# Five rearrangements at the edges of a kernel bound by TensorE: decayed attention, then a low-rank mixer and two large products

## The chip, the cores and the metric

The kernel runs on one core of a Trainium2 chip. The metric is the device time of one execution in microseconds; every time below is the median of several executions, with the range or a 95% interval where it matters. The first eight experiments ran on one chip, the last four on another, the kernel before each time in the same rounds; runs of different rounds are compared by their ratios to it, or in their traces. A profile is the record of one execution, and its span (from the first to the last instruction) is some 1.8 us shorter than the time of the same execution.

## The reference

```python
# q, k, v: (4, 8, 768, 64); lam: 8 numbers near 0.98; blocks of 64 positions
for b in range(nb):
    intra = einsum(qb, kb) * Dmask                 # lam**(i-j) for i >= j, else 0
    intra = einsum(intra, vb)
    inter = einsum(qb * lam**(pos + 1), kv_state)
    out[block] = intra + inter
    kv_state = lam**block * kv_state + einsum(kb * lam**(block-1-pos), vb)
x = out as (4, 768, 512)
u = x + V.T @ (U.T @ x)        # per batch, over the 768 positions; rank 32
result = u + relu(u @ w_ch1) @ w_ch2               # 512 -> 2048 -> 512
```

The large weights arrive as 64-bit floats, as pairs of 32-bit words, and VectorE and ScalarE turn them into 32-bit floats and then into high, low and difference parts. U and V come the same way.

## The kernel before

Attention runs in 24 steps of 128 positions (4 batches by 6, counted 0 to 23). In each step TensorE turns q and k (pq, pk), multiplies the masked scores by v (intra, into px), adds to the state (pkv), makes the scores of the next step (pss) and starts px of the next step from the state (inter). VectorE masks the scores and adds up the state kv, GpSimd scales q and k by powers of lam (qs, ks), and ScalarE copies the results of turning and of px out of PSUM. Pieces of work with the weights are dealt out to the steps as asides. The two large products, from about 163 us on, take four fifths of the time.

```python
pieces = [("prep", 0), ("scale", 0), ("scores", 0), ("inter", 0), ("masked", 0)]
for s in range(NS):
    ...
    step += [("intra", s), ("late", s), ("state", s)]
    step += [("turned", done - 1)] * (done > 0)
    step += [("scores", s + 1)] * more
    step += [("aside", s)] * (done >= 0)
    step += [("inter", s + 1), ("masked", s + 1), ("fade", s + 1)] * more
    step += [("aside", s)] * (done < 0)
...
def powers():                       # run before step 0
    ...
    for a in range(HP):
        nc.vector.tensor_tensor_scan(powq[:, a, :], lamh[:, a : a + 1].broadcast_to([P, P]),
            zeros.broadcast_to([P, P]), 1.0, ALU.mult, ALU.add)
...
def scores(s):
    for a in range(HP):             # 4 x 2 products of 64 x 128 weights
        for x in range(2):
            nc.tensor.matmul(out=pss[:, x, a, :], lhsT=kt[half[x], a, :],
                rhs=qt[half[x], a, :], start=True, stop=True)
...
for steps, at in (                  # which part of which weight in which step
    (u_side, (0, 2, 2, 3, 3)),
    (v_steps(), (1, 1, 3, 3, 4, 4, 4, 5, 5, 5)),
    (w1_steps(0, True), (3, 4, 5, 6, 7, 8, 9, 10, 12, 13, 14)),
    (w1_steps(1, True), (8, 9, 10, 11, 15, 16, 17, 18, 19, 20, 21)),
):
```

The first four entries of `w1_steps(0, True)` are four loads of one block of w_ch1; the fifth entry, step 7, begins to convert it.

## Time and profile before

| | value |
|---|---|
| time | 686.68 us, median of 3 (686.65 to 686.88) |
| span of the profiled run | 684.9 us, granted clock 0.995 |
| instructions | 12572, of which 4812 matmuls |
| attention | until about 132 us |
| largest wait of TensorE in it | 2.10 us at 33.7 us, for the state kv |
| load rate of the DMA engines, 0 to 50 us | 195 GB/s, 9.75 MB |

The prediction shows the lines that it rests on. Two readings became important only later. The first is a line from the page's table of DMA queues (queue and kind: packets, MB, share of the 16 engines' time). It counts the packets that fetch instructions:

```profile
q8 instruction: 38, 0.62, 0.4%
```

Each packet brings 16 KB of instructions; 19 of the 38 come in the first 130 us.

The second is the order of events of the kernel before (start, length, engine and line, what it does, how often; in brackets what the engine waited for):

```profile
8.03 2.22 POOL L371 TENSOR_TENSOR ks<-kraw,small 128x512 f32<-128x512 f32 x2 [6.72 <-DVE small L305]
...
14.26 2.08 PE L398 MATMUL pss<-qt,kt 64*128 64x128 f32 x16
...
16.27 0.85 PE L439 MATMUL px<-kv,qs 64*64 64x64 f32 x32
...
50.66 0.43 DVE L424 TENSOR_TENSOR kv<-pkv,faded 128x256 f32<-128x256 f32 x1 [0.94 <-PE pkv L416]
51.00 0.97 DVE L153 TENSOR_SCALAR sc<-words 128x512 uint32<-128x512 uint32 x1
```

The scans of lam's powers, 8.23 to 11.16 in the prediction's lines, stand almost wholly beside this GpSimd work. In front of inter(1) the second pss takes 2.08 instead of 1.16 us, in the half clock from 13.25 to 16.66. And at step 7, at 51.00, VectorE takes up the words of w_ch1 right behind the state: they had landed, but only at 50.77 by the trace, 0.2 us before they were wanted.

### The profile page before, as it was taken

The numbers are of one execution on the slowest core, as the hardware profiler recorded it, in microseconds if no ns is written. First come the engines' busy times: TensorE is split into PE (matmuls) and PEld (weight loads), VectorE is DVE, ScalarE is ACT, GpSimd is POOL, SyncE is SP. The second block draws the span as 40 slices with busy tenths as digits, with TensorE's granted clock in tenths as the row PEclk, the third lists the DMA queues.
The fourth block names the chain that finished last, engine by engine and source line by source line (L and its number), as shares of the span: only waits on it lengthen the run. The fifth ranks groups of instructions, "written<-read, shape, count | busy, mean of one in ns | idle before, by whom it ended". The sixth has DMA issues, their size and how long they took to land.

```text
span 684.9 us, 12572 instructions
## 1 busy us (share of the span) xinstructions
PE 675.0 (99%) x4812; PEld 547.1 (80%) x4812; DVE 499.4 (73%) x856; ACT 291.5 (43%) x543; POOL 114.1 (17%) x92
## 2 busy tenths in 40 slices
PE   8999999999999999999999999999999999999997
PEld 6878888887888888888888888888888888888885
DVE  5568898876999877777799255787586676775854
ACT  3657777644666544444456231232232322322320
POOL 3546566532000000000000000030030110300300
PEclk9999999999999999999999999999999999999999
DMA  9978886244577855655566989956353363453431
GB/s 206 208 171 218 217 214 157 78 169 169 186 256 248 266 201 206 206 203 207 194 239 236 329 301 372 331 159 193 94 193 114 105 201 95 147 166 101 156 92 62
DMA packets 131629, 131.24 MB, mean 192 GB/s; under 512 B 81330, under 2 KB 89522, under 8 KB 131570
## 3 DMA queue, kind: packets, MB, share of 16 engines
q1 hardware_dynamic: 130514, 130.18, 60.5%
q8 instruction: 38, 0.62, 0.4%
q10 hardware_dynamic: 1056, 0.26, 0.2%
q14 instruction: 21, 0.17, 0.1%
HBM read 80.09 MB, written 50.33 MB: 190 GB/s over the span
## 4 chain that ended last, share of the span: by engine, by line
PE 96%; DVE 2%; ACT 1%; issue 1%; DVEq 0%
PE pz L704 26%; PE pz L837 13%; PE pz L835 13%; PE pd L714 13%; PE pd L839 13%; PE px L451 3%; PE pss L398 3%; PE put L514 2%; PE px L439 2%; PE pq L353 1%; PE pkv L416 1%; PE pk L353 1%; PE pu L497 1%; PE pp L465 1%; PE pr L483 1%
## 5 line engine op out<-in xcount | busy, mean ns | idle before, releaser
L704 PE MATMUL pz<-u_hl,w 128*128 128x512 f32 x768 | 191.2, 398 | 0.2 <-ACT r L710 0.2
L704 PEld LDWEIGHTS pz<-u_hl,w 128*128 128x128 f32 x768 | 143.9, 188 | 36.4 <-issue 1.1
L835 PE MATMUL pz<-w_hl,m 128*128 128x512 f32 x384 | 151.6, 396 | 0.0
L837 PE MATMUL pz<-w_hl,m 128*128 128x512 f32 x384 | 151.6, 396 | 0.0
L839 PE MATMUL pd<-w_d,m 128*128 128x512 f32 x384 | 150.0, 396 | 0.0
L818 ACT ACTIVATE m<-mt 128x512 fp32r<-128x512 f32 x96 | 60.6, 632 | 196.3 <-PE pd L839 139.0
L819 DVE SCALAR_TENSOR_TENSOR m<-rm,m 128x512 fp32r<-128x512 f32 x96 | 71.4, 745 | 52.9 <-ACT m L818 52.7
L859 POOL TENSOR_TENSOR o<-o,u 128x512 f32<-128x512 f32 x20 | 29.8, 1525 | 447.5 <-DVE o L857 447.5
L719 DVE SCALAR_TENSOR_TENSOR r<-pd,r 128x512 f32<-128x512 f32 x96 | 61.8, 685 | 55.1 <-ACT r L710 45.5
L714 PE MATMUL pd<-u_d,w 128*128 128x512 f32 x384 | 98.2, 397 | 0.0
L837 PEld LDWEIGHTS pz<-w_hl,m 128*128 128x128 f32 x384 | 72.3, 188 | 17.7
L839 PEld LDWEIGHTS pd<-w_d,m 128*128 128x128 f32 x384 | 72.3, 188 | 17.7
L835 PEld LDWEIGHTS pz<-w_hl,m 128*128 128x128 f32 x384 | 72.3, 188 | 17.6
L714 PEld LDWEIGHTS pd<-u_d,w 128*128 128x128 f32 x384 | 72.2, 188 | 17.4
L710 ACT ACTIVATE r<-pz 128x512 f32<-128x512 f32 x96 | 51.9, 593 | 58.3 <-PE pz L704 58.2
L820 DVE SCALAR_TENSOR_TENSOR m<-m 128x512 fp32r<-128x512 f32 x96 | 69.1, 720 | 0.9
L817 DVE TENSOR_SCALAR mt<-rm 128x512 uint32<-128x512 uint32 x96 | 46.2, 481 | 27.2 <-DMA rm<-r_d 26.3
L204 ACT CAST w<-wt 128x512 fp32r<-128x512 f32 x32 | 19.9, 622 | 41.3 <-DVE wt L201 34.0
L407 DVE TENSOR_TENSOR sm<-pss,mask 128x512 f32<-128x512 f32 x48 | 30.7, 680 | 8.9 <-PE pss L398 8.9
L451 PEld LDWEIGHTS px<-vraw,sm 128*64 128x64 f32 x768 | 25.2, 141 | 9.1 <-issue 3.2
L382 POOL TENSOR_TENSOR qs<-qt,powq 128x512 f32<-128x512 f32 x20 | 25.5, 1277 | 33.4 <-ACT qt L356 24.9
L451 PE MATMUL px<-vraw,sm 128*64 128x64 f32 x768 | 28.7, 229 | 1.9 <-DVE sm L407 1.9
(88 smaller groups left out, 711.9 us busy)
## 6 DMA issues: line engine op xcount, KB each, us to landing
r_d<-r SPq DMA_DIRECT2D x96, 256.0 KB, 2.6
rm<-r_d SPq DMA_DIRECT2D x96, 256.0 KB, 2.7
words<-in_moe_w_ch_dram SPq DMA_DIRECT2D x30, 512.0 KB, 4.1
w_d<-w SPq DMA_DIRECT2D x16, 768.0 KB, 3.3
w_hl<-w_d SPq DMA_DIRECT2D x16, 512.0 KB, 6.2
vraw<-in_v_dram SPq DMA_DIRECT2D x24, 256.0 KB, 4.1
u_d<-x_nat SPq DMA_DIRECT2D x24, 256.0 KB, 3.4
u<-u_d SPq DMA_DIRECT2D x24, 256.0 KB, 4.1
```

The lines of the kernel that those rows point to most:

```text
L451: nc.tensor.matmul(out=px[half[t], x, a, :], lhsT=sm[:, x, a, half[t]], rhs=vr[:, 2 * a + x, :], start=(first and a == 0), stop=(a == HP - 1),
L704: nc.tensor.matmul(out=acc[g][0], lhsT=w[:, n, ct, :], rhs=uhl[g][:, n, ct, :], start=(ct == 0 and n == 0), stop=(ct == CT - 1 and n == 1),)
L710: nc.scalar.mul(rs[g], acc[g][0], 1.0 + E)
L714: nc.tensor.matmul(out=acc[g][1], lhsT=w[:, 2, ct, :], rhs=ud[g][:, ct, :], start=(ct == 0), stop=(ct == CT - 1),)
L719: nc.vector.scalar_tensor_tensor(rs[g], acc[g][1], 4096.0, rs[g], ALU.mult, ALU.add)
L817: nc.vector.tensor_scalar(t.bitcast(U32), r.bitcast(U32), HI, None, ALU.bitwise_and)
L818: nc.scalar.activation(out=m[:, 0], in_=t, func=AF.Relu)
L819: nc.vector.scalar_tensor_tensor(m[:, 1], r, 0.0, hi, ALU.max, ALU.subtract)
L820: nc.vector.scalar_tensor_tensor(m[:, 2], hi, E, low, ALU.mult, ALU.subtract)
L835: nc.tensor.matmul(out=pz, lhsT=m[:, 0, cols], rhs=hl[:, 0], start=first, stop=False)
L837: nc.tensor.matmul(out=pz, lhsT=m[:, 1, cols], rhs=hl[:, 1], start=False, stop=end)
L839: nc.tensor.matmul(out=pd, lhsT=m[:, 2, cols], rhs=dd, start=first, stop=end)
```

## The change

The intent is to take TensorE's waits and overhead out of the attention part, in five places. (1) lam is loaded first, and its powers, which only step 1 needs, are computed behind the mask of step 0. (2) U moves one or two steps forward, so that its conversions no longer stand in front of V's. (3) ScalarE's conversions of weights stand a step later everywhere, behind the copies that TensorE waits for. (4) Scores are made on 64x64 instead of 64x128 tiles, so that they and inter, which follows them, are in the same tiling mode. (5) The last sum and its store are done in two halves.

```diff
-                nc.tensor.matmul(
-                    out=pss[:, x, a, :], lhsT=kt[half[x], a, :], rhs=qt[half[x], a, :],
-                    start=True, stop=True,
-                )
+                for t in range(2):
+                    nc.tensor.matmul(
+                        out=pss[half[t], x, a, :], lhsT=kt[half[x], a, half[t]],
+                        rhs=qt[half[x], a, :], start=True, stop=True,
+                    )
     pieces = [("prep", 0), ("scale", 0), ("scores", 0), ("inter", 0), ("masked", 0)]
+    pieces += [("powers", 0)]
-        step += [("intra", s), ("late", s), ("state", s)]
-        step += [("turned", done - 1)] * (done > 0)
+        step += [("intra", s)] + [("late", s)] * (done < 0) + [("state", s)]
+        step += [("turned", done - 1)] * (done > 0) + [("late", s)] * (done >= 0)
-        (u_side, (0, 2, 2, 3, 3)),
-        (v_steps(), (1, 1, 3, 3, 4, 4, 4, 5, 5, 5)),
+        (u_side, (-1, 1, 1, 2, 2)),
+        (v_steps(), (0, 0, 3, 3, 4, 4, 5, 5, 5, 5)),
-        late[:] = [None] * (s < NT)
+        late[:] = [None]
+    nc.scalar.dma_start(out=lam_row[:, 0:H], in_=lam.unsqueeze(0))
     load_next("q", nc.sync)
     load_next("k", nc.scalar)
-    for name in "qkvkvqkv":
+    for name in "qkvkv":
+        load_next(name)
+    aside(-1)
+    for name in "qkv":
         load_next(name)
...  (two conversions of w_ch1 put into the late list; blank matmuls before and behind lam's product)
-        finish(NG - 1, n)
+        finish(NG - 1, n, [slice(0, C // 2), slice(C // 2, C)] if n == TG - 1 else [slice(0, C)])
```

More of the change, by code (lines that the diff above doesn't have):

```diff
@@ L203, in five @@
             )
-            nc.scalar.copy(o[:, 0, :], t)
+            on_scalar(lambda: nc.scalar.copy(o[:, 0, :], t))
         def six():
@@ L208, in six @@
             nc.vector.tensor_tensor(out=w, in0=w, in1=st["t"], op=ALU.subtract)
-            nc.scalar.mul(st["o"][:, 1, :], w, 4096.0)
+            on_scalar(lambda: nc.scalar.mul(st["o"][:, 1, :], w, 4096.0))
         def seven():
@@ L270, in load @@
             )
-            if name == "q" and s == 0 and h == 0:
-                engine.dma_start(out=lam_row[:, 0:H], in_=lam.unsqueeze(0))
         raw[s, name] = t
@@ L335, with keep_busy @@
     half = [slice(0, D), slice(D, P)]
-    def keep_busy():
+    def keep_busy(n, cols=P):
         out = one_bank([P, C], "idle", "pq")
-        for i in range(5):
-            nc.tensor.matmul(out=out[:, 0:P], lhsT=blank, rhs=blank, start=True, stop=True)
+        for i in range(n):
+            nc.tensor.matmul(
+                out=out[:, 0:cols], lhsT=blank, rhs=blank[:, 0:cols], start=True, stop=True
+            )
     qts, kts = {}, {}
@@ L360, in prep @@
             for name in "qk":
-                if (s, a0, name) != (0, 0, "q"):
-                    turn_half(s, a0, name)
+                turn_half(s, a0, name)
         st[s].update(qt=qts.pop(s), kt=kts.pop(s))
@@ L397, in scores @@
             for x in range(2):
-                nc.tensor.matmul(
-                    out=pss[:, x, a, :], lhsT=kt[half[x], a, :], rhs=qt[half[x], a, :],
-                    start=True, stop=True,
-                )
+                for t in range(2):
+                    nc.tensor.matmul(
+                        out=pss[half[t], x, a, :], lhsT=kt[half[x], a, half[t]],
+                        rhs=qt[half[x], a, :], start=True, stop=True,
+                    )
     def masked(s):
@@ L650 @@
     make_gather()
-    keep_busy()
-    turn_half(0, 0, "q")
+    keep_busy(2)
     pl = one_bank([P, H], "pl", "pt")
     nc.tensor.matmul(out=pl, lhsT=lam_row[:, H:], rhs=lam_row[:, 0:H], start=True, stop=True)
+    keep_busy(3)
     nc.vector.tensor_copy(out=lamb, in_=pl)
@@ L657 @@
     scale_k(0)
-    powers()
-    run.update(aside=aside, late=on_scalar_late)
+    run.update(aside=aside, late=on_scalar_late, powers=lambda s: powers())
     for what, s in pieces:
@@ L847, in residual, with finish @@
             nc.sync.dma_start(out=us[n], in_=u_d[g * TG + n])
-    def finish(g, n):
+    def finish(g, n, parts=[slice(0, C)]):
         pz, pd = acc.pop(n)
@@ L856, in finish @@
             nc.scalar.mul(o, pz, 1.0 + E)
-        nc.vector.scalar_tensor_tensor(o, pd, 4096.0, o, ALU.mult, ALU.add)
-        if g < NG - 1:
-            nc.gpsimd.tensor_tensor(out=o, in0=o, in1=u, op=ALU.add)
         s = g * TG + n
         b, c = divmod(s, NT)
-        nc.sync.dma_start(out=out[b, c * P : (c + 1) * P, :], in_=o)
+        for part in parts:
+            nc.vector.scalar_tensor_tensor(
+                o[:, part], pd[:, part], 4096.0, o[:, part], ALU.mult, ALU.add
+            )
+            if g < NG - 1:
+                nc.gpsimd.tensor_tensor(out=o, in0=o, in1=u, op=ALU.add)
+            nc.sync.dma_start(out=out[b, c * P : (c + 1) * P, part], in_=o[:, part])
     def ahead(i):
```

## The prediction

> **What bounds the kernel now.** I read first the page's busy shares and the chain that ended last, because they say whether there is one bound or several.
>
> ```profile
> PE 675.0 (99%) x4812; PEld 547.1 (80%) x4812; DVE 499.4 (73%) x856; ACT 291.5 (43%) x543; POOL 114.1 (17%) x92
> ...
> PE 96%; DVE 2%; ACT 1%; issue 1%; DVEq 0%
> ```
>
> TensorE is the bound nearly everywhere; only some 4% of the chain, 27 us, lies elsewhere. The two large products (L704, L714, L835 to L839: 79% of the chain) run without a gap from about 163 us on, and the diff leaves their instructions in their order on every engine: I compared the lists of both kernels, and they differ in the attention part, which ends near 132 us, and in the last two outputs. So I read only two places closely: the first 132 us and the last 5.
>
> In order of time, TensorE's rows of one undisturbed step of attention and then of the disturbed step behind it (start, length, group):
>
> ```profile
> 28.20 1.16 PE L398 MATMUL pss<-qt,kt 64*128 64x128 f32 x16
> 29.29 0.69 PE L439 MATMUL px<-kv,qs 64*64 64x64 f32 x32
> 29.92 0.66 PE L353 MATMUL pq<-ident,qraw 128*128 128x128 f32 x4
> 30.41 0.60 PE L353 MATMUL pk<-ident,kraw 128*128 128x128 f32 x4
> 30.94 1.15 PE L451 MATMUL px<-vraw,sm 128*64 128x64 f32 x32
> 31.92 0.64 PE L416 MATMUL pkv<-vraw,ks 128*64 128x64 f32 x16
> 32.49 1.16 PE L398 MATMUL pss<-qt,kt 64*128 64x128 f32 x16
> 35.76 0.69 PE L439 MATMUL px<-kv,qs 64*64 64x64 f32 x32 [2.10 <-DVE kv L424]
> 36.38 0.66 PE L353 MATMUL pq<-ident,qraw 128*128 128x128 f32 x4
> 36.88 0.80 PE L353 MATMUL pk<-ident,kraw 128*128 128x128 f32 x4
> 37.61 1.98 PE L451 MATMUL px<-vraw,sm 128*64 128x64 f32 x32
> 39.51 1.64 PE L398 MATMUL pss<-qt,kt 64*128 64x128 f32 x16
> ```
>
> From 28.20 to 32.49 every group starts as the one before it drains: 4.29 us, all TensorE. Then comes the largest hole of the kernel: inter (L439) waits for the state kv. And from 37 us px takes 1.98 instead of 1.15 us. The view by stretches of 1 us gives a granted clock of 0.57 in 37 to 38, 0.50 in 38 to 40 and 0.72 in 40 to 41. Why kv was late, VectorE's rows show:
>
> ```profile
> 31.39 1.43 DVE L153 TENSOR_SCALAR sc<-words 64x384 uint32<-64x384 uint32 x1
> 32.74 1.21 DVE L154 TENSOR_SCALAR m<-words 64x384 uint32<-64x384 uint32 x1
> 33.98 1.29 DVE L170 SCALAR_TENSOR_TENSOR m<-words,m 64x384 f32<-64x384 uint32 x1
> 35.20 0.41 DVE L424 TENSOR_TENSOR kv<-pkv,faded 128x256 f32<-128x256 f32 x1
> ```
>
> The pkv that kv waits for was complete near 32.5; three conversions of V stood in front of it, right behind two of U. And the beginning:
>
> ```profile
> 6.37 2.08 PE L398 MATMUL pss<-qt,kt 64*128 64x128 f32 x16
> 8.23 2.93 DVE L314 TENSOR_TENSOR_SCAN powq<-small 128x128 f32<-128x128 f32 x4
> 11.08 1.25 DVE L407 TENSOR_TENSOR sm<-pss,mask 128x512 f32<-128x512 f32 x2
> 11.30 1.27 POOL L382 TENSOR_TENSOR qs<-qt,powq 128x512 f32<-128x512 f32 x1 [1.05 <-DVE powq L314]
> ```
>
> The first scores are complete at 8.45, but their masking waits until 11.08 behind the powers of lam. Inter(1) then starts at 16.27.
>
> **What the Trainium skill says.** (1) "TensorEngine Tiling (Array Packing)", Tiling Modes, Key Properties: changing the tiling mode drains TensorE. The trace agrees: within pss pairs of records start 0.112 us apart, but from its last pair to inter, which is in another mode, it is 0.202; from intra to pkv, the same mode, 0.052, the ordinary spacing. (2) "TensorE: Matmul & The Clock Gate", LDWEIGHTS: loading weights takes time by columns, P/1.2 ns, so 107 ns for 128 and 53 for 64. The trace agrees: the second pair of pss starts 0.102 later than the steady spacing, the second four of inter 0.049. (3) The same page, Part 1: the clock is judged in free-running windows of 3413 ns, half speed after an idle one. The trace's clock records have just such pieces: half speed from 13.25 to 16.66 and from 37.14 to 40.55, after windows with some 1.9 and 2.0 us without matmuls, so an entirely idle window was not needed. (4) "SBUF — State Buffer", Who interferes with whom: a two-port VectorE operation, or one with two SBUF inputs, and GpSimd lock each other out for a whole instruction. It agrees: the L153 above took 1.43 us for 384 columns beside GpSimd work that began at 31.33 (qs), while U's, 192 columns with GpSimd idle, took 0.25.
>
> **Part by part.**
>
> *Scores on 64x64 tiles.* 16 records of 64x128 weights become 32 of 64x64; two tiles running side by side become four. Each tile still streams 128 columns eight times, so the floor of 8 x 0.112 = 0.89 us stays. What goes is overhead. Before, start of pss to start of inter: 7 x 0.112 + 0.102 + 0.202 = 1.09 (measured 1.092). After: 8 x 0.112 + 0.049 = 0.945, since inter is now in the same mode; and inter's own first weights no longer stand alone, 0.049 less. Together 0.147 + 0.049 = 0.196. Of the 23 scores after the first, s=1 will wait for something else (below), three are followed by no inter and save only about 0.102 - 0.049 = 0.053, 19 save all: 19 x 0.196 + 3 x 0.053 = 3.9 us. VectorE is 80 to 90% busy in that stage, so some of the faster steps will wait for a mask or state; I choose to take off 0.3: **-3.6**.
>
> *U and V spread thinner.* U moves one to two steps forward, V's first pair stays behind masked(4) but without U before it. The hole cost 2.18 us of waiting (3.267 - 1.092), and the half clock behind it 0.92 for intra (1.906 against 0.982), 0.20 for the transposes (1.224 against 1.024) and 0.48 for pss (1.572 against 1.092): 3.8. After: VectorE starts V's sc near 30.65 instead of 31.39, on free ports: two of some 0.35, until 31.4. Then GpSimd's qs takes the ports until 32.7, and the third (about 0.55 by its width) ends near 33.3. So kv comes near 33.7 for an inter ready at 33.4: 0.3 to 0.5 remain, too short for a cold window: **-3.3**. The additional early load, 0.2 MB, is 0.9 us at the 210 GB/s of the first 24 us; the loads run about two steps ahead there, so I count nothing.
>
> *Powers behind the first mask.* The lam row now goes first, so the mask is ready near 6.5 instead of 7.94. But two blank matmuls, the lam product and three more blank ones stand before the transposes: six records of 0.213 after a lam row landing near 2.8, so the transposes begin near 4.6 instead of 3.69 and pss(0) near 6.65. Its data are complete near 8.8, masked(0) runs 8.85 to 10.15: 2.2 us sooner. Now powq waits: 0.4 of small operations and 2.93 of scans give 13.5, then qs(1), 1.27, so inter(1) starts near 14.9 instead of 16.27: 1.4 sooner, while TensorE, done with pss(1) near 12.75, waits 2.1 us. That hole lies across the windows ending at 13.25 and 16.66; the second would hold 1.6 us without matmuls, near what made others cold. A cold window costs about 1.6 us, as above. I give it 6 in 10, so -1.4 + 0.6 x 1.6: **-0.4**.
>
> *ScalarE's conversions late.* A gap of 0.59 at 54.8 (intra to pkv took 1.568 instead of 0.982), and one of 0.2 near 96.8, come of exponents that waited 1.30 us for VectorE in front of faded and the copies. Moved a step later they wait no more, but stand in a step with te and u_hl: 0.59 x 3 + 0.63 + 0.61 + 1.06 + 1.44 = 5.5 us of ScalarE in a step of some 4.75, so I leave about 0.3 of each: **-0.2**. Against it, the four casts of V (0.52 each) are now together behind intra(6), two more than before in front of faded and the next copies, whose slack was 0.42 (kt copied at 49.48, pkv at 49.90): 1.04 - 0.42, **+0.6**.
>
> *Last sums by halves.* The last sum ends at 681.71 and its 256 KB store is complete at 683.79. Two halves of about 0.42 end 0.1 later, but only half of the 0.78 us of packets stands behind the second: **-0.2**.
>
> Sum: -3.6 - 3.3 - 0.4 - 0.2 + 0.6 - 0.2 = -7.1, and 686.7 - 7.1 = 679.6. As I rounded against the change at several places, I say **679.4 us**.
>
> **Rivals.** First, *a wait takes the place of the one removed*: VectorE or ScalarE binds in the faster steps, and most of the scores' 3.9 us go to waits for masks. For it: VectorE's slices of 0.8 and 0.9. Against it: in the undisturbed step sm ends near 30.70, intra starts at 30.94, and of that margin the new order uses about 0.1. It would make 682 to 683. Second, *a cold window in the beginning after all, and another at step 5 or 6* where V's casts now stand: 1.6 us each, 681 to 682. Third, *everything works and the first hole stays warm*: -1.4 from the powers, -3.8 from the hole, -3.9, no loss at V's casts: 676 to 677. Fourth, the 64x64 records don't run four abreast, because tiles of one row half write one bank: pss would grow to 1.7 us or more and cost over 12 us. Against it: inter does run four abreast (four records within 0.02 us, groups 0.058 apart) onto the same banks in just this arrangement. I give it 1 in 50.
>
> **Range and chances.** The scores' part is certain to about 0.8, the hole to 0.6, the clock in the beginning to 1.0, the rest to 0.6; together some 1.6, and eight in ten is about 1.3 of that, a little more downwards: 676.9 to 681.6. A gain of 2% would need 672.9, beyond every part at its best; a loss of 2% needs something broken.
>
> **What would show it.** pss of 32 records with fours 0.112 apart and 0.945 from its start to inter's; no VectorE wait over 0.5 at 30 to 36 us and no half clock there; masked(0) near 8.9, powq's last scan near 13.5, inter(1) near 14.9; the second scores waiting for nothing; pkv near step 7 waiting for a copy of kt. The prediction is wrong if the fours are not 0.112 apart, if a hole as long appears at another step, or if TensorE's time from 163 us on changes at all.

## The result

| | before | after |
|---|---|---|
| time, median of 4 | 686.66 us (686.57 to 686.88) | 680.11 us (677.06 to 680.53) |
| ratio | | 0.9894, 95% interval 0.9866 to 0.9923 |
| span and clock of the profiled run | 684.9 us, 0.995 | 678.7 us, 0.997 |

A ratio is the mean time of one kernel's fast runs over that of the other's in the same rounds, so it is not quite the ratio of the medians. 680.11 lies 0.7 us from the predicted 679.4 and inside the range. The runs of the kernel after spread over 3.5 us, those of before over 0.3 (in the later rounds, with 11 and 12 runs, over 1.4 to 2.3).

The page after (engine: busy us, share, instructions; the instruction queue; the chain that ended last, by engine):

```profile
PE 668.4 (98%) x5196; PEld 543.0 (80%) x5196; DVE 495.8 (73%) x857; ACT 291.5 (43%) x543; POOL 114.6 (17%) x92
...
q8 instruction: 41, 0.67, 0.4%
...
PE 97%; DVE 1%; DMA 1%; issue 0%; POOL 0%; SPq 0%; ACT 0%; DVEq 0%; POOLq 0%
```

TensorE has 384 matmuls more, and as many weight loads, 768 instructions in all; three more packets of instructions are fetched. In the chain a share of DMA is new.

The beginning, in order of time (a choice of rows):

```profile
7.93 1.29 DVE L407 TENSOR_TENSOR sm<-pss,mask 128x512 f32<-128x512 f32 x2 [2.06 <-PE pss L398]
9.51 1.37 DVE L312 TENSOR_TENSOR_SCAN powq<-small 128x128 f32<-128x128 f32 x4
11.03 1.27 POOL L381 TENSOR_TENSOR qs<-qt,powq 128x512 f32<-128x512 f32 x1 [2.91 <-ACT x_nat L456]
12.35 0.69 PE L439 MATMUL px<-kv,qs 64*64 64x64 f32 x32 [0.54 <-POOL qs L381]
```

The mask comes at 7.93 instead of 11.08, the four scans take 1.37 instead of 2.93 us, and inter(1) starts at 12.35 instead of 16.27.

TensorE in an undisturbed step, and VectorE's state behind the third conversion of V:

```profile
24.08 1.10 PE L398 MATMUL pss<-qt,kt 64*64 64x128 f32 x32
25.01 0.64 PE L439 MATMUL px<-kv,qs 64*64 64x64 f32 x32
...
28.15 1.10 PE L398 MATMUL pss<-qt,kt 64*64 64x128 f32 x32
```
```profile
27.11 1.57 DVE L170 SCALAR_TENSOR_TENSOR m<-words,m 64x384 f32<-64x384 uint32 x1
28.61 0.41 DVE L424 TENSOR_TENSOR kv<-pkv,faded 128x256 f32<-128x256 f32 x1
```

From pss to inter it is 0.93 instead of 1.09 us, and from one pss to the next 4.07 instead of 4.29. The state behind the conversion of V comes 0.5 us after its pss starts; before, it came 2.7 us after it. That hole is gone: inter(5) waits 0.08 us. But three steps later (TensorE, then VectorE):

```profile
38.73 0.56 PE L439 MATMUL px<-kv,qs 64*64 64x64 f32 x20
39.71 0.45 PE L439 MATMUL px<-kv,qs 64*64 64x64 f32 x12 [0.42 <-issue]
...
45.83 0.47 PE L497 MATMUL pu<-vp 128*128 128x512 f32 x1
49.92 0.34 PE L451 MATMUL px<-vraw,sm 128*64 128x64 f32 x4 [3.61 <-DVE sm L407]
...
52.19 1.99 PE L398 MATMUL pss<-qt,kt 64*64 64x128 f32 x32
```
```profile
48.50 0.43 DVE L153 TENSOR_SCALAR sc<-words 128x512 uint32<-128x512 uint32 x1 [4.89 <-DMA words<-in_moe_w_ch_dram]
```

Three new things are to be seen. In the middle of inter(7), between its records 20 and 21, TensorE stands still and waits for nothing ("issue"): 0.42 us by the view. From the start of inter to what follows it takes 1.36 us instead of 0.575, so the pause costs 0.79. Then intra(8) waits 3.61 us for a mask; VectorE, which has the mask to do, waits 4.89 us for the words of w_ch1. And behind this hole a pss takes 1.99 instead of 1.10 us: in the stretches from 52 to 54 us the granted clock is 0.50.

Both traces compared at the start of each intra, and at the ends, give the account (after minus before, us):

| stretch | shift | what lies in it |
|---|---|---|
| start to intra(1) | -4.08 | lam, powers |
| intra(1) to intra(4) | -0.26 | scores -0.22 a step, one pause in pkv(2) +0.40 |
| intra(4) to intra(6) | -3.82 | hole of 2.18 and half clock gone, scores |
| intra(6) to intra(7) | +0.58 | pause in inter(7) |
| intra(7) to intra(8) | +3.62 | hole at the words of w_ch1, +3.68; scores |
| intra(8) to intra(9) | +1.15 | half clock behind the hole, +1.96; scores; a wait of 0.59 gone |
| intra(9) to the first product | -3.15 | scores, ScalarE |
| the products and the end | -0.17 | halves |
| sum | -6.13 | span 684.88 to 678.75 |

So the right sum was reached with a larger gain in the beginning, and with losses that the prediction does not contain.

### The profile page after: what moved, and what is told of

Read it like the earlier page. It is cut to its first block, busy times and chain, and to the rows that moved or that the text cites. A ratio compares the mean times of both kernels' runs of the same rounds, so it can differ in the third digit from the quotient of the medians.

```text
span 678.7 us, 13340 instructions
## 1 busy us (share of the span) xinstructions
PE 668.4 (98%) x5196; PEld 543.0 (80%) x5196; DVE 495.8 (73%) x857; ACT 291.5 (43%) x543; POOL 114.6 (17%) x92
## 4 chain that ended last, share of the span: by engine, by line
PE 97%; DVE 1%; DMA 1%; issue 0%; POOL 0%; SPq 0%; ACT 0%; DVEq 0%; POOLq 0%
PE pz L708 27%; PE pz L841 13%; PE pz L839 13%; PE pd L718 13%; PE pd L843 13%; PE px L451 4%; PE pss L398 4%; PE put L514 2%; PE pq L353 2%; PE pk L353 1%; PE px L439 1%; PE pkv L416 1%; PE pu L497 1%; DMA words<-in_moe_w_ch_dram 1%; PE pp L465 1%; PE pr L483 1%
## 5 line engine op out<-in xcount | busy, mean ns | idle before, releaser
L451 PEld LDWEIGHTS px<-vraw,sm 128*64 128x64 f32 x768 | 24.6, 138 | 11.2 <-DVE sm L407 6.4
```

Of the source, the lines that this page charges most:

```text
L451: nc.tensor.matmul(out=px[half[t], x, a, :], lhsT=sm[:, x, a, half[t]], rhs=vr[:, 2 * a + x, :], start=(first and a == 0), stop=(a == HP - 1),
```

## The experiments

Twelve runs were made, one of them of the kernel after itself, all with correct results. The before of the first four was 686.38 us, of the next four 686.36, of the last four 686.27.

### One part of the change at a time, on the kernel before

**scores_only.** The diff is the first hunk shown above.

> The kernel before with only the scores on 64x64 tiles. If the tiles' saving is as worked out (0.196 us for each of 19 steps, 0.053 for three) and TensorE binds at every step: 3.9 us faster, 682.8, with pss to inter 0.92 to 0.95 us apart in the warm steps. If the bytes of the first 50 us bind (the rival): the steps before step 8 save nothing, because the words of the first block of w_ch1 come no sooner; then about 2.7 us, near 684. If VectorE's masks bind: under 2 us.

Measured: 683.57 us (682.36 to 684.87), ratio 0.9962 (0.995 to 0.9974). In the trace each undisturbed step is 0.219 us shorter, from its pss to inter 0.924 and from inter to what follows 0.575 instead of 0.626. But the steps are no longer undisturbed everywhere: TensorE pauses in mid-group twice, ending at 31.28 and 65.35 us. The trace of the kernel before has no such pause. The part is worth 2.6 us (0.0038 of 686.4). The trace shows 3.50, in part because this run had full clock from 10.43 to 34.33 us and so escaped the half clock of the beginning: intra(1) starts 1.74 us sooner than in the kernel before, of which the tiles are 0.22.

**spread_only.**

```diff
-        (u_side, (0, 2, 2, 3, 3)),
-        (v_steps(), (1, 1, 3, 3, 4, 4, 4, 5, 5, 5)),
+        (u_side, (-1, 1, 1, 2, 2)),
+        (v_steps(), (0, 0, 3, 3, 4, 4, 5, 5, 5, 5)),
-    for name in "qkvkvqkv":
+    for name in "qkvkv":
+        load_next(name)
+    aside(-1)
+    for name in "qkv":
```

> The kernel before with only U and V moved forward. If the hole of 33 to 36 us and its cold window go and nothing else comes: 3.3 to 3.8 us faster, about 683. If the bytes bind: the hole goes, but another comes at step 8 behind the words of w_ch1 (in the kernel before, the first of those conversions starts at 51.0 us when some 9.85 MB have landed), so the gain is under 1.5 us unless the clock stays warm, 685 to 686.5.

Measured: 683.83 us (683.23 to 684.5), ratio 0.9967 (0.9954 to 0.9979), 2.3 us. In the trace the hole at 33 us and its cold window go, -4.17 by intra(6), and from intra(7) to intra(8) 0.68 comes back: pkv(7) waits 0.46 us for the copy of kt, behind V's four casts. No hole appears at the words of w_ch1: with the stage only 3.5 us earlier the words are there (landed at 47.36, taken up at 47.50).

**powers_only.** The move of the powers, the load of lam in front, and the blank matmuls (2, lam's product, 3).

> The kernel before with the powers behind the first mask, the lam row first and the blank matmuls split, and no more. Inter(1) should start near 12.4 us instead of 16.27, as in the changed kernel. If that is kept to the end: 3.9 us faster, near 682.8; if the old hole at step 4 (33 us) stays at its length but ends 3.9 sooner, this holds. If the bytes bind at step 8: the 3.9 are given back there in part, and the total is 0 to 2 us faster, 684.5 to 686.7.

Measured: 682.12 us, runs of 681.31 to 683.48 and one of 688.14, ratio with all of them 0.9954 (0.9928 to 0.9981). In the trace -4.13 by intra(1), and -5.22 at the end. The profiled run happened to have no cold window behind the hole at 33 us, which accounts for the rest. The cold window of the beginning, to which the prediction gave 6 in 10, did not come. At step 7, here 5.6 us earlier than before, VectorE already waits 0.86 us for the words of w_ch1, though no mask is late yet.

**moved_only.** Only the powers are moved, nothing about lam.

```diff
+    pieces += [("powers", 0)]
-    powers()
-    run.update(aside=aside, late=on_scalar_late)
+    run.update(aside=aside, late=on_scalar_late, powers=lambda s: powers())
```

> The kernel before with only the powers behind the first mask; lam row, blank matmuls and the transposes as before. If the scans took 2.93 us in the kernel before because GpSimd's ks stood on the shared port beside them, and 1.37 in the changed kernel because ks was over by then: here they start near 9.9 and ks ends near 10.25, so they take 1.4 to 1.8, qs(1) starts near 11.8 and inter(1) near 13.1. If the scans have another reason to be slow (the first use, the lam row): 2.9 again, inter(1) near 14.5. Time 682.5 to 684.5 in the first case, 684 to 686 in the second.

Measured: 683.48 us (682.16 to 683.7), ratio 0.9956 (0.9943 to 0.9968); in the trace -3.27 by intra(1), -3.25 at the end. The order of time of its beginning:

```profile
8.01 2.08 POOL L371 TENSOR_TENSOR ks<-kraw,small 128x512 f32<-128x512 f32 x2 [6.70 <-DVE small L305]
...
10.32 1.37 DVE L314 TENSOR_TENSOR_SCAN powq<-small 128x128 f32<-128x128 f32 x4
```

GpSimd's ks ends at 10.09, and the scans behind it take 1.37 us, the same instructions that took 2.93 beside ks. So most of the beginning's gain comes of the move alone, and 1.56 us of it, which the prediction did not have, is a duration that was no constant. The move also ends the half clock of the beginning: of the four traces with the old beginning three have it (before, late_only, spread_only), of the ten with moved powers none. By scores_only it is worth some 1.5 us (an estimate, 1.74 - 0.22), and it is contained in the 3.27 here and in the 4.08 of the kernel after.

**late_only.** ScalarE's conversions into the late list, the late list behind the copies, one step later.

```diff
-            nc.scalar.copy(o[:, 0, :], t)
+            on_scalar(lambda: nc.scalar.copy(o[:, 0, :], t))
-            nc.scalar.mul(st["o"][:, 1, :], w, 4096.0)
+            on_scalar(lambda: nc.scalar.mul(st["o"][:, 1, :], w, 4096.0))
-        step += [("intra", s), ("late", s), ("state", s)]
-        step += [("turned", done - 1)] * (done > 0)
+        step += [("intra", s)] + [("late", s)] * (done < 0) + [("state", s)]
+        step += [("turned", done - 1)] * (done > 0) + [("late", s)] * (done >= 0)
-        late[:] = [None] * (s < NT)
+        late[:] = [None]
```

> The kernel before with only ScalarE's conversions late from step 7 on. The prediction gave this part 0.2 us: 686.0 to 686.4, with the gap of 0.59 us at step 8 (intra to pkv) under 0.3. If it does nothing: no difference from the kernel before.

Measured: 685.83 us (685.06 to 685.94), ratio 0.9991 (0.9978 to 1.0004). The interval holds 1, so no gain is shown in time; in the trace it is 0.75 us, 0.64 of it where pkv had waited 0.59 at 54.8 us.

The four parts give 2.6 + 2.3 + 3.2 (powers_only) + 0.6 = 8.7 us by their ratios, with the halves' 0.2 some 8.9. All together the change gives 7.3 (0.0106 of 686.66). The parts together give some 1.6 us less than apart; as the half-widths of the four intervals, taken as independent, come to 2.3 us, these ratios alone do not show a loss. The traces do.

### The words of w_ch1 and the pauses

**w1_later.** The kernel after, with the conversion of w_ch1 begun one step later; the loads stay where they are.

```diff
-        (w1_steps(0, True), (3, 4, 5, 6, 7, 8, 9, 10, 12, 13, 14)),
+        (w1_steps(0, True), (3, 4, 5, 6, 8, 9, 10, 11, 12, 13, 14)),
```

> The changed kernel, with the seven conversion steps of the first block of w_ch1 a step later where there is room (steps 8 to 14 in place of 7 to 14); its loads stay at steps 3 to 6. Theory that the hole of 3.7 us at step 8 is VectorE standing at words that have not landed: the hole goes or shrinks under 0.5, the half clock behind it (2.0 us) goes too, and the time falls by 3 to 5.7 us from 680.1 to 674.4 to 677. Rival that the queue of loads itself is late, q, k and v included: the hole moves to another step and the time stays above 679.

Measured: 679.18 us (676.65 to 681.29), ratio 0.9894 (0.9877 to 0.9912). The hole at intra(8) is gone from the trace, but the time does not show it: the ratio is that of the kernel after, and the 3 to 5.7 us that the expectation gave the hole did not come. TensorE's rows at inter(7):

```profile
41.22 0.54 PE L439 MATMUL px<-kv,qs 64*64 64x64 f32 x20
42.95 0.45 PE L439 MATMUL px<-kv,qs 64*64 64x64 f32 x12 [1.18 <-issue]
```

The pause stands at the same record of the program as in the kernel after, between records 20 and 21, and is nearly three times as long by the view. Four more pauses end at 21.19, 30.96, 52.92 and 96.25 us. Before each of the five a packet of instructions ends, 1.27 to 1.57 us earlier (41.68 for the pause ending at 42.95). In the stretch in which that packet travels, the loads alone keep the DMA engines full.

**w1_loads_later.** Both blocks' loads two or three steps later as well, to relieve the DMA engines.

```diff
-        (w1_steps(0, True), (3, 4, 5, 6, 7, 8, 9, 10, 12, 13, 14)),
-        (w1_steps(1, True), (8, 9, 10, 11, 15, 16, 17, 18, 19, 20, 21)),
+        (w1_steps(0, True), (6, 7, 8, 9, 10, 11, 12, 13, 14, 15, 16)),
+        (w1_steps(1, True), (10, 11, 12, 13, 15, 16, 17, 18, 19, 20, 21)),
```

> The changed kernel, with loads and conversions of the first block of w_ch1 three steps later (loads at steps 6 to 9, conversions at 10 to 16), of the second two (loads at 10 to 13). Theory that the loads of the first 50 us, some 212 GB/s without a pause, bind the steps: no wait of VectorE for words, and instruction fetches (which stand among those loads) land sooner, so pauses shrink to under 1 us in all: 674 to 677. Rival that the fetches are late for another reason than the loads: the hole at step 8 is gone but pauses of 1 us and more stay, 677 to 680.

Measured: 680.32 us (678.27 to 682.92), ratio 0.9915 (0.9894 to 0.9935). The hole at step 8 is gone here too, but two pauses in mid-group are there (ending at 25.99 and 42.71 us), and the first block is now converted in steps 10 to 16, in 15 and 16 beside the second: masks come late at 64.8, 90.9 and 96.6 us, and from intra(10) to intra(18) 1.6 of the 5.56 us gained are lost. Waits were exchanged, not removed, and the time lies above both ranges of the expectation.

**no_scores.** The kernel after with the scores on 64x128 tiles again.

> The changed kernel with the scores back on 64x128 tiles. Theory that the 64x64 scores cost pauses of TensorE in mid-group, because their 768 more instructions are fetched too late: no pause inside a group of 0.26 us or more in the first 130 us besides those that the kernel before has too, while the changed kernel pauses 0.36 us in pkv of step 2 and 0.63 in inter of step 7. The hole at step 8 stays, some 1.5 us shorter, as TensorE comes there later. Sum: 3.9 lost, 0.9 of pauses and about 1.5 of hole won, so 1 to 2 us slower than the changed kernel, 681 to 682. Rival that the pauses come from something else in the attention (the casts of V, late loads): they stay where they are.

Measured: 683.63 us (681.72 to 684.74), ratio 0.9967 (0.9953 to 0.9982), some 2 us more than expected: between intra(7) and intra(8) 3.38 us are lost, so the hole did not become 1.5 us shorter. Its trace has no pause at all, and the hole at step 8 is still there. VectorE:

```profile
47.65 0.84 DVE L153 TENSOR_SCALAR sc<-words 128x512 uint32<-128x512 uint32 x1 [3.66 <-DMA words<-in_moe_w_ch_dram]
```

So the hole does not come of the tiles: it comes of everything being earlier while the loads are not. The tiles are what brings the pauses.

**no_scores_w1_later.** Both edits, 64x128 tiles and the conversion a step later.

> The same with the first block of w_ch1 converted a step later. If the hole at step 8 is the words' arrival and the pauses are the scores' instructions, both are gone: shift of 4.1 from the powers, 2.2 and 1.4 from the hole of 33 us, 0.2 from the end, less 0.5 at V's casts: about 7.4 us under the kernel before, 679. If the hole only moves on, above 681.

Measured: 679.42 us (678.96 to 679.95), ratio 0.9901 (0.9888 to 0.9913). Against no_scores, in the same rounds, the later conversion gives 683.63 - 679.42 = 4.2 us: without pauses the hole has its full price, and the range is 1.0 us instead of 3.0. With the hole away, what the prediction saw at V's casts becomes visible (TensorE, step 7):

```profile
42.80 0.69 PE L415 MATMUL pkv<-vraw,ks 128*64 128x64 f32 x16 [0.46 <-ACT kt L356]
```

From intra(7) to intra(8) the trace loses 0.68 us against the kernel before.

### A version that keeps what was gained

**scores_from_9.** w1_later, and 64x64 tiles only from step 9 on, where the loads have become thinner.

```diff
-                for t in range(2):
+                for rows in half if s >= 9 else [slice(0, P)]:
                     nc.tensor.matmul(
-                        out=pss[half[t], x, a, :], lhsT=kt[half[x], a, half[t]],
+                        out=pss[rows, x, a, :], lhsT=kt[half[x], a, rows],
                         rhs=qt[half[x], a, :], start=True, stop=True,
                     )
```

> The changed kernel with the words of w_ch1 converted a step later, and the scores on 64x64 tiles only from step 9 on, when the loads no longer fill the DMA engines. If the tiles are worth 0.2 us a step and their pauses come of instruction fetches behind those loads: the shift of the version without them (7.4 us in its profile, 679.4) and 0.22 for each of some 13 steps, so 676 to 677, with at most one pause of 0.3 us. If the pauses come of the number of instructions alone: pauses of 0.6 us and more at later steps, 678 to 680.

Measured: 677.10 us (676.85 to 678.26), ratio 0.987 (0.9857 to 0.9884). No pause and no hole in its trace, which is 9.79 us shorter than that of the kernel before, clock 1.000 in all runs.

**scores_from_9_v.** The same with V's fifth part back in step 4: `(v_steps(), (0, 0, 3, 3, 4, 4, 4, 5, 5, 5))`.

> The same, with the first step of V's split at step 4 again, so that two of V's four casts come a step earlier on ScalarE. If the wait for the copy of kt near step 7 (0.68 us from step 7 to 8 in the version without the tiles) comes of four casts in a row: 0.4 to 0.7 us faster than the run before it. If not: the same within 0.3, or slower by a wait at step 5.

Measured: 677.43 us (676.31 to 677.59), ratio 0.9868 (0.9855 to 0.9882). In the trace pkv(7) no longer waits (0.00 instead of 0.68 from intra(7) to intra(8)); in time the two kernels can't be told apart, so the 0.4 to 0.7 us expected did not come.

**after_again.** The kernel after once more, unchanged, in these rounds.

> The changed kernel unchanged, beside the versions above on one chip. Its runs spread from 677.1 to 680.5 before; if the spread comes of where the clock's windows fall, runs with a granted clock of 1.0 lie near 677 and those below 0.998 near 680.

Measured: 678.31 us (675.83 to 680.84), ratio 0.9884 (0.9861 to 0.9907). Six runs of one program spread over 5.0 us, and the clock does not sort them: 680.38 and 675.99 both ran at 1.000. In the profiled run the pause in inter(7) is 1.5 us long by the view and the hole at step 8 2.2 us, with full clock from 8.96 us on. So the expectation that the clock alone tells 677 from 680 fell. scores_from_9 beats the kernel before clearly; of its lead over the kernel after, 0.9 us in the means (677.33 against 678.27), none is certain, as the intervals overlap. What sets it apart is steadiness, 1.4 us of range in four runs against 5.0 in six.

## Why the prediction was right

The number was right, but two steps of its working failed with opposite signs, and the other parts came out nearly as worked out. By its own steps:

**Scores on 64x64 tiles: right.** Predicted 0.945 from pss to inter and 0.196 a step; measured 0.924 and 0.219. The three steps without inter gained 0.057 each, predicted 0.053. The fours run 0.109 to 0.110 apart at full clock, so the fourth rival (four tiles not abreast) is out. Gross that is 19 x 0.219 + 3 x 0.057 = 4.3 us, and the two pauses of the profiled run, 0.40 and 0.79, leave 3.1. The prediction had 3.9 less 0.3 for waits on masks; the deduction was needed, but for another reason.

**U and V spread thinner: right.** Predicted -3.3. From intra(4) to intra(6) the kernel after gains 3.82; without the scores' 0.22 and 0.06 that is 3.5. The third conversion did run beside GpSimd, 1.57 us, and kv was in time.

**Powers behind the first mask: this step failed.** It said "0.4 of small operations and 2.93 of scans give 13.5, then qs(1), 1.27, so inter(1) starts near 14.9", and it added six tenths of a cold window, hence -0.4. The runs show -4.08. Three terms were mis-sized. The scans took 1.37: 1.56 us sooner, shown by moved_only. The mask came at 7.93 instead of 8.85: 0.92, from lam landing earlier (its product stands at 2.20, estimated 2.8) and from a clock that was warm at 7.22 instead of 9.83 us, which is a matter of luck, as it first warms up anywhere from 4.6 to 11.2 us in these traces. These two are 2.48 of the 2.55 us by which inter(1) was early. And the 0.6 x 1.6 = 0.96 for a cold window falls away: TensorE's wait there was 0.54 us instead of 2.1. The odds of 6 in 10 were read off the edges 13.25 and 16.66 of one trace, but they lie elsewhere in other traces, at 10.43 in scores_only and 11.40 in spread_only. The step's error is 3.7 us. That the scan would be slow beside GpSimd could have been asked of the profile: the prediction used just this reading for V's conversions, and took the scans' 2.93 from the same kind of overlap as a constant.

**"The loads run about two steps ahead there, so I count nothing": this step failed.** It was read from the first 24 us, and it is what the hole at step 8 contradicts. In the kernel after VectorE is free for the words at 43.61 us; before, it took them up at 51.00, so the work is 7.4 us earlier, where the words had a margin of 0.2. The loads could not follow: over the first 50 us they move 210 GB/s against 195 before, and by 48 us 9.88 MB have landed, what before had by 51. In the list of the loads' issues the cause is plain: from 25.0 to 49 us the kernel after issues them back to back, and the last block of words goes out at 44.16, landing at 48.5; before, gaps of 1.0 to 1.9 us lie between the issues, waits for buffers to come free, and the block went out at 46.47, in time for 51.00. The hole takes 3.68 us between the starts of two groups that follow each other in 0.41 elsewhere; the half clock behind it costs 1.96, which is the 1.15 of the account with the scores' 0.22 and a wait of 0.59 that lay there before: 5.6 us in the profiled run. w1_later and no_scores_w1_later take the hole away in the trace, and the pair no_scores and no_scores_w1_later prices it in time at 4.2 us. With the tiles in the early steps it has no price in time that shows, since the pauses take its place: after and w1_later have the same ratio.

**Pauses: not foreseen.** They appear in the five traces whose tiles are 64x64 in the first nine steps (after, after_again, scores_only, w1_later, w1_loads_later), in mid-group and with no semaphore named (after_again and w1_loads_later have one more of the kind in front of a group, 0.37 and 1.13 us), and in none of the nine others. They are waits for instructions, and the kept traces show it. Number TensorE's instructions (matmuls, weight loads and its own semaphore instructions) in order of start: all twelve pauses in mid-group and the two in front of a group stand at a number that leaves 193 or 194 when divided by 256. Packets come as often, one for every 256: 9739 of these instructions and 38 packets before, 10219 and 40 in scores_from_9, 10507 and 41 after. And in none of the fourteen traces does TensorE pass such a boundary less than 1.2 us behind the end of a packet; at the fourteen pauses it goes on 1.25 to 1.57 us behind one, while the kernel before always has 1.92 us or more. The tiles bring the boundaries closer together: in the kernel after they pass at 19.75, 24.14 and 28.42 us, in the kernel before at 20.82, 25.42 and 31.23. A pause is long where its packet sets off late: 4.45 us behind the boundary before it for the 0.42 us in the kernel after, 5.58 for the 1.49 in after_again, and never more than 2.63 in the first 20 packets of the nine traces without pauses. Why a packet sets off late stays open; that it queues behind loads would fit.

**ScalarE's conversions late, and V's casts.** Predicted -0.2 and +0.6. Alone, the first gave -0.75 in the trace and no certain gain in time. The second is 0.68 in the trace of no_scores_w1_later and spread_only, with pkv waiting for kt at step 7 as predicted; in the kernel after it lay hidden behind the pause, 0.05 us.

**Halves: right.** Predicted -0.2; between the last matmul and the end of the span the kernel after gains 0.20.

**The sum.** In the profiled run: scores -4.33, hole at 33 us -3.54, powers -4.08, ScalarE -0.85 (the wait of 0.59, and 0.26 later), casts +0.05, halves -0.20, the hole at step 8 with its half clock +5.64, pauses +1.19: together -6.1, where the spans differ by 6.13. Against the prediction's -7.1 the powers gave 3.7 more and the other four parts 2.1 more, on which it had "rounded against the change"; the two things it did not contain took 6.8. That these nearly cancel is chance, and it is no better founded by the medians: the profiled run was the slowest of the four, 680.53.

Of the rivals, the first was right in that a wait took the place of the one removed, but it named masks and not words; the second's cold window came, at step 8 instead of in the beginning; the third, 676 to 677 if every gain stays, is close to what scores_from_9 reaches by another way, 677.10. By the prediction's own test, "wrong if ... a hole as long appears at another step", its mechanism was wrong at that point, and the total is no proof of the working.

## What to carry to other kernels

When a change pulls a stage forward, look up for each consumer in it when its data were issued and landed, over the whole stage and not its first part, and move the consumer back by as much as the loads can't follow. A duration read beside a busy neighbour is not a property of the instruction: ask what else ran, and whether it will run there again. And when an edit multiplies small instructions in a stage whose DMA queues are full, try it only in the steps where they aren't, and judge by spread as well as by median. This rests on the two traces of scores_from_9 and its variant; with the tiles everywhere, two pauses fell later too, at 65.35 us in scores_only and at 96.25 in w1_later.

## What the Trainium skill lacked or had wrong

- "Runtime: NRT & Kernel Launch", Instruction fetch mechanics, says that instructions are fetched in blocks of 16 KiB by the sequencer's own DMA queue and that crossing a block is mostly hidden. The packets of 16 KB are in the trace, one for every 256 instructions of TensorE. Beside full loads the crossing was not hidden here: pauses of up to 1.49 us by the view, all at such a crossing and ending 1.25 to 1.57 us after a packet's end.
- "SBUF — State Buffer", Who interferes with whom, has the rule that explains it, but its list of operations doesn't name the scan: four scans of 128 columns took 2.93 us beside GpSimd and 1.37 behind it.
- "TensorE: Matmul & The Clock Gate", Part 1, says that the clock falls after an idle window of about 3.4 us (a later paragraph lets short idle stretches between groups do it too, without a figure). The window before the half clock at 51.59 us held 1.41 us of matmuls (3.41 less 1.74 and 0.26 of waiting), and it was enough to fall. The window in front of it, 44.77 to 48.18, held 1.54 and was followed by full clock; no run here shows where the limit lies.
